# Row halves of the matrix array for the kv products, their turn and the turn of the feature sums; two closing adds on GpSimd; three gathers moved ahead of a scatter

## The chip, the cores and the metric

The kernel runs on one core of a Trainium2 chip. The metric is the device time of one execution in microseconds, less is better. The core has TensorE (PE for its products, PEld for its weight loads), VectorE (DVE), ScalarE (ACT), GpSimd (POOL) and SyncE (SP), each with its own instruction queue in order.

## The reference

Random feature attention over 8 batches, 8 heads, 576 positions and 64 columns a head, then a mixture of 8 experts that takes for each of the 4608 tokens the one with the largest cosine to the token.

```python
def phi(x):                                   # 128 features, cos and sin
    proj = np.einsum('bhsd,md->bhsm', x, omega)
    return np.concatenate([np.cos(proj), np.sin(proj)], axis=-1) / np.sqrt(m)
q_p, k_p = (phi(q), phi(k))
kv = np.einsum('bhsm,bhsd->bhmd', k_p, v)     # (features x 64) for each head
z = np.sum(k_p, axis=2)                       # sum of each feature over the positions
num = np.einsum('bhsm,bhmd->bhsd', q_p, kv)
den = np.einsum('bhsm,bhm->bhs', q_p, z)      # then clamped away from zero
x = num / den                                 # rows of 512, one for each token
...
logits = xn @ en.T / tau                      # cosine with 8 expert vectors
expert_idx = np.argmax(logits, axis=1)
out[mask] = gate_w[mask, None] * (np.maximum(x[mask] @ w1[e], 0.0) @ w2[e])
```

## The kernel before

**Attention.** It goes in 32 steps n = 0 to 31, each for one batch and two heads (hh = 0 in partitions 0 to 63, hh = 1 in 64 to 127). The 576 positions are 9 chunks of 64. Everything is float32 here. The order of the work in a step is written out by hand in the loop `for n in range(NS)`, and each engine follows it in order; a step's products for step n are mixed with the numerators of step n - 1 and the projections of step n + 1. TensorE's order in the loop is: `proj_q(n)` (L235, L244 and one block of L218), `z_turn(n-1)` (L340), `kv_turn(n-1)` (L326), `proj_k(n+1)` (L218), `num(n-1)` (L371), `turns(n)` (L181), `kv_products(n)` (L306).

`kv_products` multiplies v (64 positions x 64 columns, the loaded weights) with the sines and cosines of k (`sck`: 64 positions x features; sines in half 0, cosines in half 1). Head hh takes rows 64 hh to 64 hh + 63 of the array. Eight of the nine chunks take both halves in one product of 256 columns; even chunks go to output columns 0 to 63 of the array and odd ones to 64 to 127, so that the sum over all chunks is in two parts. The last chunk is split in products of 128 columns. VectorE copies the result from PSUM (`kv_copy`, L316, 128 x 512). `kv_turn` loads 128 x 128 of that copy as weights and multiplies by `rmat`, which adds the two parts and appends the products with the 8 expert vectors.

The feature sums z: GpSimd adds the chunks of each half in `zsum` (L293 on 128 x 512, L295 on 128 x 256), down to two blocks and the ninth chunk, and `z_turn` (L340) adds these three over the positions with products against a matrix of ones: three products of 128 rows for each half, accumulated, with one column of result for each head. `kv_out` (L350, L353) copies both results to SBUF for `num`.

ScalarE rounds, takes absolute values, sines and copies (L262, L273, L283, L204 or L209). VectorE takes the fractions (L266), the absolute value of q's (L277), the copies from PSUM and the division of `num` (`norm`), and pieces of the routing in the steps from 9 on (`pieces`). GpSimd takes `zsum`, the issue of one piece of the expert weights each step (`weights_in`, 32 pieces, L92 and L98), the cast of the result (`to_rows`, L403), sums and squares (`sums` L449, `squares` L408). SyncE issues the loads of q, k, v and the stores of the rows. Tiles with one buffer tie these together: the `zs` tile of `zsum` is free again when `z_turn` has read it, and `kv_products` writes to the PSUM region `kreg` that the projection of k for the next step was read from.

**Experts.** 43 blocks of 128 tokens, each of one expert. The first 11 blocks are made from the tokens of the first four batches while the attention still runs, the other 32 after all logits are known; the token numbers of these (`prm`, L737) are ready in block j = 7. In the loop over j, TensorE does `hidden(j+1)` (L882, 32 products), the turn of a gathered block (`turn_x`, L824) and `result(j)` (L903, 8 products). `result(j)` ends with the scatter of the block's rows to the output, an indirect DMA that GpSimd issues (L916) after ScalarE has scaled the rows (L915). `gather(t)` (L782) is an indirect DMA too, issued by GpSimd after that; in block 7 these are the gathers of blocks 11, 12 and 13.

Of the kernel before, what the change touches and what calls it, by code (L numbers as in the profile page):

```python
# [11 lines left out]
FP32 = mybir.dt.float32  # L12
# [5 lines left out]
ALU = mybir.AluOpType  # L18
# [10 lines left out]
def kernel(  # L29
# [12 lines left out]
    nc = tc.nc  # L42
# [6 lines left out]
    P = 128  # L49
# [5 lines left out]
    NCH = S // 64  # L55
# [8 lines left out]
    W = 64 + E + 1  # L64
# [56 lines left out]
    pref = persist.tile([P, E], BF16)  # L121
    tri = persist.tile([P, E, E], FP32)
    sm = persist.tile([P, 12, E], FP32)
    ones2 = persist.tile([P, 2], FP32)
    pio2 = persist.tile([P, 1], FP32)
    sel = persist.tile([P, SG, E], BF16)
    pm = persist.tile([P, SG], BF16)
# [4 lines left out]
    with tc.tile_pool(name="psA", bufs=1, space=PSUM) as psA, tc.tile_pool(  # L132
# [9 lines left out]
        st = {}  # L142
# [144 lines left out]
        def zsum(n, half):  # L287
            d = st[n]
            t = d["sck"][:, half]
            if half == 1:  # L290
                d["z"] = pa.tile([P, 6, P], FP32, tag="zs", name="zs", bufs=1)
            z = d["z"]
            nc.gpsimd.tensor_tensor(z[:, 0:4], t[:, 0:4], t[:, 4:8], ALU.add)  # L293
            r = z[:, 4 * half : 4 * half + 2]
            nc.gpsimd.tensor_tensor(r, z[:, 0:2], z[:, 2:4], ALU.add)  # L295
            d[f"z{half}"] = (r[:, 0], r[:, 1], t[:, 8])

        def kv_products(n):
            d = st[n]
            parts = [(c, c % 2, 0, 2) for c in range(NCH - 1)]  # L300
            parts += [(NCH - 1, half, half, half + 1) for half in range(2)]
            for c, grp, a0, a1 in parts:
                for hh in range(2):
                    r0 = 64 * hh
                    at = 512 * hh + P * a0
                    nc.tensor.matmul(  # L306
                        kreg[64 * grp : 64 * grp + 64, at : at + P * (a1 - a0)],
                        lhsT=d["v"][r0 : r0 + 64, c],
                        rhs=d["sck"][r0 : r0 + 64, a0:a1, KS[c]],
                        start=(c < 2),  # L310
                        stop=(c == NCH - 1),
                    )

        def kv_copy(n):
            t = pa.tile([P, 2, 2 * P], FP32, tag="kvT", name="kvT", bufs=1)
            nc.vector.tensor_copy(  # L316
                t, kreg[:, 0:1024].rearrange("p (h m) -> p h m", h=2)[:, :, 0 : 2 * P]
            )
            st[n]["kvT"] = t

        def kv_turn(n):
            b, i = steps[n]
            d = st[n]
            for hh in range(2):
                for half in range(2):
                    nc.tensor.matmul(  # L326
                        nm2[:, half, hh * W : hh * W + W - 1],
                        lhsT=d["kvT"][:, hh, half * P : half * P + P],
                        rhs=rmat[:, i, hh],
                        start=True,  # L330
                        stop=True,
                    )

        ZC = 486

        def z_turn(n):
            for half in range(2):
                parts = st[n][f"z{half}"]
                for j, z in enumerate(parts):
                    nc.tensor.matmul(  # L340
                        nm2[:, 0, ZC + 2 * half : ZC + 2 * half + 2],
                        lhsT=z,
                        rhs=ones2,
                        start=(j == 0),
                        stop=(j == len(parts) - 1),
                    )

        def kv_out(n):
            kv = pa.tile([P, 2, 2, W], FP32, tag="kv", name="kv", bufs=1)
            nc.vector.tensor_copy(  # L350
                kv[:, :, :, W - 1], nm2[:, 0, ZC : ZC + 4].rearrange("p (a h) -> p a h", a=2)
            )
            nc.vector.tensor_copy(  # L353
                kv[:, :, :, 0 : W - 1],
                nm2[:, :, 0 : 2 * W].rearrange("p a (h w) -> p a h w", h=2)[:, :, :, 0 : W - 1],
            )
            st[n]["kv"] = kv
# [118 lines left out]
        load_kq(-1)  # L476
        load_v(0)
        make_identity(nc, ident)
        nc.vector.memset(ones2, 0.0)
        for hh in range(2):  # L480
            nc.vector.memset(ones2[64 * hh : 64 * hh + 64, hh : hh + 1], 1.0)
        nc.vector.memset(half1, 0.5)
        nc.vector.memset(pio2, PI_2)
        for par in range(2):
# [524 lines left out]
        def weights_in(n):  # L1009
            if n < 4 * E:  # L1010
                emit_weight_piece(n)

        weights_in(0)
        for n in range(NS):
# [34 lines left out]
                whole_turns(n + 1, "k")  # L1049
            if n < NS:  # L1050
                zsum(n, 1)
                weights_in(n + 1)
                fold(n, "q")
                wave(n, "si", "k")
            if nx:
# [4 lines left out]
            if n < NS:  # L1060
                wave(n, "co", "q")
                zsum(n, 0)
            if nx:
                if pieces.get(n):
                    copy_kq(n)
                else:
                    copy_k(n)
                    copy_q(n)
                if n + 2 < NS:
                    load_kq(n + 1)  # L1070
# [52 lines left out]
        square_sums(NS - 1)  # L1123

        r2 = {}
        QUIET = 7

        def route_second_pe(j):
            if j == 1:
# [62 lines left out]
        for j in range(NBLK):  # L1192
# [8 lines left out]
                gate_end(t)  # L1201
            for t in gates_at.get(j, []):
                gate_shift(t)
            result(j)
            route_second_pe(j)
            for t in gathers_at.get(j, []):
                gather(t)


# [33 lines left out]
```

## Time and profile before

| what | value |
|---|---|
| time, median of 3 runs | 536.39 us (535.89 to 536.85) |
| time of the profiled execution | 535.86 us |
| its span, first to last instruction | 534.1 us |
| PE, PEld busy | 510.4, 409.6 us |
| DVE, ACT, POOL busy | 349.8, 356.3, 324.1 us |
| mean granted TensorE clock | 0.985 |

The profiled execution's time is 1.8 us more than its span. Busy time is the sum over all stages; the 32 steps of the attention, the 43 blocks of the experts and the change between them have different limits, so the rows below are cut by stage.

### The profile page before, as it was taken

To read this page: it belongs to the slowest core of one execution; us is meant where nothing else is said; L and a number is where in the kernel's file an instruction comes from. 1 tells how busy PE (TensorE), PEld (TensorE's weight loads), DVE (VectorE), ACT (ScalarE), POOL (GpSimd) and SP (SyncE) were. 2 spreads that over 40 slices of the span, in tenths; PEclk is the share of its full clock that TensorE was granted. 3 is DMA by queue.
4 is the path that set the end of the run, shared out by engine and by line. 5 is a ranking of instruction groups with operands and counts; after the bars stand their busy time and mean duration, and the time that the engine had idled before them with its cause. 6 is when DMAs were issued, how large, how long until landed. Compare 5 with 4: busy or idle time off the path is not lost.

```text
span 534.1 us, 17479 instructions
## 1 busy us (share of the span) xinstructions
PE 510.4 (96%) x7244; PEld 409.6 (77%) x7244; DVE 349.8 (66%) x756; ACT 356.3 (67%) x466; POOL 324.1 (61%) x374
## 2 busy tenths in 40 slices
PE   6799999999999999999999999989988999999993
PEld 4588888878888887888778878877766677777772
DVE  4468866786766688888878778858934444444440
ACT  5687877888788788878877888746633343333431
POOL 3357666665866566667677676876653655556422
PEclk9799999999999999999999999999998999999997
DMA  6655777677668858766866677524232323233110
GB/s 148 147 119 120 151 169 154 124 161 168 139 138 159 180 121 155 173 142 124 177 158 136 124 170 156 97 49 107 80 110 73 111 78 114 84 105 106 52 50 0
DMA packets 57885, 65.81 MB, mean 123 GB/s; under 512 B 29637, under 2 KB 37829, under 8 KB 57808
## 3 DMA queue, kind: packets, MB, share of 16 engines
q0 software_dynamic: 18304, 31.11, 29.0%
q1 hardware_dynamic: 39200, 33.51, 24.0%
q8 instruction: 58, 0.95, 0.7%
q14 instruction: 19, 0.16, 0.1%
q10 hardware_dynamic: 304, 0.08, 0.1%
HBM read 68.08 MB, written 16.16 MB: 158 GB/s over the span
## 4 chain that ended last, share of the span: by engine, by line
PE 87%; issue 4%; POOL 2%; ACT 2%; DVE 2%; another core or an unknown queue 1%; DMA 1%; POOLq 0%; ACTq 0%
PE ps L371 14%; PE ps L882 13%; PE ps L306 13%; PE ps L903 10%; PE ps L340 9%; PE ps L218 8%; PE ps L235 7%; PE ps L181 6%; PE ps L326 6%; PE ps L824 2%; POOL out_dram L916 1%; DMA w_sb<-in_omega_dram 1%; DVE sck L266 0%; ACT sck L283 0%
## 5 line engine op out<-in xcount | busy, mean ns | idle before, releaser
L293 POOL TENSOR_TENSOR zs<-sck 128x512 f32<-128x512 f32 x64 | 81.6, 1275 | 92.0 <-PE ps L326 58.7
L882 PEld LDWEIGHTS <-w_sb 128*128 x1376 | 81.7, 99 | 12.3 <-issue 3.2
L882 PE MATMUL ps<-kq,w_sb 128*128 128x128 f16 x1376 | 85.6, 221 | 1.8 <-DVE kq L818 1.0
L903 PE MATMUL ps<-w_sb,late 128*128 x344 | 81.9, 379 | 2.0 <-issue 2.0
L371 PE MATMUL ps<-kv,siq 128*64 128x73 f32 x1152 | 76.5, 229 | 0.8 <-DVE kv L353 0.6
L371 PE MATMUL ps<-kv,coq 128*64 128x73 f32 x1152 | 74.9, 226 | 0.0
L894 DVE TENSOR_SCALAR late<-ps 128x512 f16<-128x512 f32 x34 | 23.5, 692 | 69.2 <-PE ps L882 38.8
L371 PEld LDWEIGHTS ps<-kv,siq 128*64 128x64 f32 x1152 | 59.8, 135 | 4.8 <-ACT sck L283 0.8
L262 ACT ACTIVATE sck<-ps 128x1152 f32<-128x1152 f32 x32 | 36.2, 1132 | 37.8 <-issue 34.5
L371 PEld LDWEIGHTS ps<-kv,coq 128*64 128x64 f32 x1152 | 60.4, 137 | 0.0
L218 PEld LDWEIGHTS ps<-omT,kqT 64*128 64x128 f32 x576 | 45.1, 196 | 18.9 <-issue 15.6
L903 PEld LDWEIGHTS <-late 128*128 128x128 f16 x344 | 31.8, 98 | 33.1 <-issue 3.1
L782 POOL DMA_INDIRECT xin_all<-rf_x,prm x43 | 44.2, 1028 | 12.5 <-issue 9.8
L218 PE MATMUL ps<-omT,kqT 64*128 64x128 f32 x576 | 51.1, 292 | 0.6 <-DVE kqT L199 0.6
L295 POOL TENSOR_TENSOR zs<-zs 128x256 f32<-128x256 f32 x64 | 48.5, 758 | 5.0
L262 ACT ACTIVATE siq<-ps 128x1152 f32<-128x1152 f32 x32 | 36.2, 1130 | 17.8 <-PE ps L244 17.8
L266 DVE SCALAR_TENSOR_TENSOR siq<-siq,ps 128x1152 f32<-128x1152 f32 x32 | 43.0, 1345 | 2.9 <-ACT siq L262 2.9
L266 DVE SCALAR_TENSOR_TENSOR sck<-sck,ps 128x1152 f32<-128x1152 f32 x32 | 42.9, 1342 | 2.4 <-ACT sck L262 2.4
L916 POOL DMA_INDIRECT out_dram<-siq,prm x21 | 22.2, 1056 | 36.0 <-ACT siq L915 30.2
L916 POOL DMA_INDIRECT out_dram<-late,prm x22 | 23.8, 1081 | 32.7 <-ACT late L915 26.9
L306 PE MATMUL ps<-sck,v 64*64 64x256 f32 (+1 forms) x680 | 38.9, 373 | 2.9 <-ACT coq L283 1.8
L283 ACT ACTIVATE coq<-coq,pio 128x1152 f32<-128x1152 f32 x32 | 39.9, 1247 | 2.5 <-DVE coq L277 2.5
(191 smaller groups left out, 1093.4 us busy)
## 6 DMA issues: line engine op xcount, KB each, us to landing
w_sb<-in_moe_w_dram POOLq DMA_DIRECT2D x32, 512.0 KB
kq<-in_k_dram SPq DMA_DIRECT2D x64, 144.0 KB, 4.1
kq<-in_q_dram SPq DMA_DIRECT2D x64, 144.0 KB, 4.5
v<-in_v_dram SPq DMA_DIRECT2D x34, 144.0 KB, 4.6
rf_x<-xb SPq DMA_DIRECT2D x32, 144.0 KB, 4.2
xin_all<-in_v_dram SPq DMA_DIRECT2D x30, 144.0 KB, 3.7
xin_all<-rf_x,prm POOLq DMA_INDIRECT x43
out_dram<-late,prm POOLq DMA_INDIRECT x22
```

Of the source, the lines that this page charges most:

```text
L218: nc.tensor.matmul(kreg[:, s * P : s * P + P], lhsT=t[r0 : r0 + 64, j * P : j * P + P], rhs=omT[r0 : r0 + 64], start=True, stop=True,)
L262: nc.scalar.activation(si, REG[nm], AF.Copy, bias=CMAGIC, scale=1.0)
L266: nc.vector.scalar_tensor_tensor(out=si, in0=si, scalar=CMAGIC, in1=REG[nm], op0=ALU.subtract, op1=ALU.subtract)
L293: nc.gpsimd.tensor_tensor(z[:, 0:4], t[:, 0:4], t[:, 4:8], ALU.add)
L295: nc.gpsimd.tensor_tensor(r, z[:, 0:2], z[:, 2:4], ALU.add)
L306: nc.tensor.matmul(kreg[64 * grp : 64 * grp + 64, at : at + P * (a1 - a0)], lhsT=d["v"][r0 : r0 + 64, c], rhs=d["sck"][r0 : r0 + 64, a0:a1 ...
L340: nc.tensor.matmul(nm2[:, 0, ZC + 2 * half : ZC + 2 * half + 2], lhsT=z, rhs=ones2, start=(j == 0), stop=(j == len(parts) - 1),)
L371: nc.tensor.matmul(nm2[r0 : r0 + 64, a, (c - c0) * W : (c - c0) * W + W], lhsT=ph[:, s * P + r0 : s * P + r0 + 64], rhs=d["kv"][:, half, h ...
L782: ins = nc.gpsimd.indirect_dma_start(out=t, out_offset=None, in_=x_rows[:], in_offset=bass.IndirectOffsetOnAxis(ap=prm[:, j : j + 1], axis=0),
L882: nc.tensor.matmul(h_ps[:, f * P : f * P + P], lhsT=weights(k), rhs=d["xT"][:, c * P : c * P + P], start=(c == 0), stop=(c == 3),)
L903: nc.tensor.matmul(y_ps, lhsT=d["hT"][:, c * P : c * P + P], rhs=weights(NW1 + c), start=(c == 0), stop=(c == NW2 - 1),)
L916: ins = nc.gpsimd.indirect_dma_start(out=out[:], out_offset=bass.IndirectOffsetOnAxis(ap=prm[:, j : j + 1], axis=0), in_=y, in_offset=None ...
```

## The change

- `kv_products`: each half of the features is a product of its own, 128 columns wide, for all nine chunks; half 0 goes to output columns 0 to 63 and half 1 to 64 to 127. 36 products in place of 20, and the sum over the chunks is complete in PSUM.
- `kv_copy` copies 128 x 256 in place of 128 x 512. `kv_turn` takes 64 rows of it (one half) as weights, four products as before, each on one half of the array's rows.
- `zsum_tail`, new, on GpSimd: two adds on 128 x 256 that fold the two blocks and the ninth chunk of both halves into one block a half. `z_turn` then takes four products of 64 rows and one column in place of six of 128 rows and two columns, each for one head and one half. The ones are one column in place of two, set with one instruction in place of three.
- `weights_in(n+1)` is issued on GpSimd's queue behind the second `zsum` and the tail in place of behind the first `zsum`.
- In block j = 7 the gathers of blocks 11 to 13 are issued ahead of `result(7)`, and so of its scatter.

```diff
         def zsum(n, half):
             ...
             nc.gpsimd.tensor_tensor(r, z[:, 0:2], z[:, 2:4], ALU.add)
-            d[f"z{half}"] = (r[:, 0], r[:, 1], t[:, 8])
+
+        def zsum_tail(n):
+            z = st[n]["z"]
+            r = z[:, 0:5:4]
+            nc.gpsimd.tensor_tensor(r, r, z[:, 1:6:4], ALU.add)
+            nc.gpsimd.tensor_tensor(r, r, st[n]["sck"][:, :, 8], ALU.add)
 
         def kv_products(n):
             d = st[n]
-            parts = [(c, c % 2, 0, 2) for c in range(NCH - 1)]
-            parts += [(NCH - 1, half, half, half + 1) for half in range(2)]
-            for c, grp, a0, a1 in parts:
-                for hh in range(2):
-                    r0 = 64 * hh
-                    at = 512 * hh + P * a0
-                    nc.tensor.matmul(
-                        kreg[64 * grp : 64 * grp + 64, at : at + P * (a1 - a0)],
-                        lhsT=d["v"][r0 : r0 + 64, c],
-                        rhs=d["sck"][r0 : r0 + 64, a0:a1, KS[c]],
-                        start=(c < 2),
-                        stop=(c == NCH - 1),
-                    )
+            for c in range(NCH):
+                for half in range(2):
+                    for hh in range(2):
+                        r0 = 64 * hh
+                        nc.tensor.matmul(
+                            kreg[64 * half : 64 * half + 64, 512 * hh : 512 * hh + P],
+                            lhsT=d["v"][r0 : r0 + 64, c],
+                            rhs=d["sck"][r0 : r0 + 64, half, KS[c]],
+                            start=(c == 0),
+                            stop=(c == NCH - 1),
+                        )
 
         def kv_copy(n):
-            t = pa.tile([P, 2, 2 * P], FP32, tag="kvT", name="kvT", bufs=1)
+            t = pa.tile([P, 2, P], FP32, tag="kvT", name="kvT", bufs=1)
...
         def kv_turn(n):
             ...
+                    r0 = 64 * half
                     nc.tensor.matmul(
                         nm2[:, half, hh * W : hh * W + W - 1],
-                        lhsT=d["kvT"][:, hh, half * P : half * P + P],
-                        rhs=rmat[:, i, hh],
+                        lhsT=d["kvT"][r0 : r0 + 64, hh],
+                        rhs=rmat[r0 : r0 + 64, i, hh],
...
         def z_turn(n):
+            z = st[n]["z"]
             for half in range(2):
-                parts = st[n][f"z{half}"]
-                for j, z in enumerate(parts):
+                for hh in range(2):
+                    r0 = 64 * hh
                     nc.tensor.matmul(
-                        nm2[:, 0, ZC + 2 * half : ZC + 2 * half + 2],
-                        lhsT=z,
-                        rhs=ones2,
-                        start=(j == 0),
-                        stop=(j == len(parts) - 1),
+                        nm2[:, hh, ZC + half : ZC + half + 1],
+                        lhsT=z[r0 : r0 + 64, 4 * half],
+                        rhs=ones1[r0 : r0 + 64],
+                        start=True,
+                        stop=True,
                     )
...
                 zsum(n, 1)
-                weights_in(n + 1)
                 fold(n, "q")
...
                 zsum(n, 0)
+                zsum_tail(n)
+                weights_in(n + 1)
...
+            if j == FOUND:
+                for t in gathers_at[j]:
+                    gather(t)
             result(j)
             route_second_pe(j)
-            for t in gathers_at.get(j, []):
-                gather(t)
+            if j != FOUND:
+                for t in gathers_at.get(j, []):
+                    gather(t)
```

## Rows read from the trace of the kernel before

**Rows 1.** The page: span, and busy time of each engine.

```profile
span 534.1 us, 17479 instructions
...
PE 510.4 (96%) x7244; PEld 409.6 (77%) x7244; DVE 349.8 (66%) x756; ACT 356.3 (67%) x466; POOL 324.1 (61%) x374
```

**Rows 2.** Busy times in a window: steps 1 to 30, from `z_turn` to `z_turn`.

```profile
core 0: us, PE busy (x) PEld busy (x) DVE busy (x) ACT busy (x) POOL busy (x), PEclk, DMA share, GB/s
26.77:341.86 315.09, 313.96 (x4971) 262.44 (x4969) 241.54 (x390) 260.38 (x240) 213.41 (x245) 1.00 0.70 147
```

**Rows 3.** Timeline of one step: start us, us, engine, line, count [idle before].

```profile
253.23 2.17 PE L306 MATMUL ps<-sck,v 64*64 64x256 f32 x40
...
253.51 0.76 POOL L295 TENSOR_TENSOR zs<-zs 128x256 f32<-128x256 f32 x1
...
255.34 1.13 PE L235 MATMUL ps<-kqT,omT 64*128 64x512 f32 x4
...
255.77 0.68 DVE L316 COPY kvT<-ps 128x512 f32<-128x512 f32 x1
...
256.62 0.61 PE L340 MATMUL ps<-ones,zs 128*128 128x2 f32 x4
...
257.95 0.97 PEld L326 LDWEIGHTS ps<-rmat,kvT 128*128 128x128 f32 x8
...
259.00 1.16 PE L218 MATMUL ps<-omT,kqT 64*128 64x128 f32 x16
...
260.09 0.35 PE L371 MATMUL ps<-kv,siq 128*64 128x73 f32 x4
...
260.26 1.13 ACT L262 ACTIVATE sck<-ps 128x1152 f32<-128x1152 f32 x1 [1.19 <-issue]
...
263.67 0.66 PE L306 MATMUL ps<-sck,xin_all 64*64 64x256 f32 x8
```

**Rows 4.** Timeline of PE in two short windows inside one `proj_k`.

```profile
259.21 0.95 PE L218 MATMUL ps<-omT,kqT 64*128 64x128 f32 x14
...
259.55 0.61 PE L218 MATMUL ps<-omT,kqT 64*128 64x128 f32 x8
```

**Rows 5.** Timeline of PE in two short windows, end of one `kv_products`.

```profile
255.01 0.40 PE L306 MATMUL ps<-sck,v 64*64 64x128 f32 x8
...
255.12 0.29 PE L306 MATMUL ps<-sck,v 64*64 64x128 f32 x4
```

**Rows 6.** Groups by line on GpSimd: busy us, mean ns | idle before.

```profile
L293 POOL TENSOR_TENSOR zs<-sck 128x512 f32<-128x512 f32 x64 | 81.6, 1275 | 92.0 <-PE ps L326 58.7 <-ACT sck L283 33.0
L295 POOL TENSOR_TENSOR zs<-zs 128x256 f32<-128x256 f32 x64 | 48.5, 758 | 5.0
...
L449 POOL TENSOR_TENSOR la<-la,xa 128x72 f32<-128x72 f32 x24 | 8.4, 352 | 0.0
```

**Rows 7.** Busy times in windows of one step (columns as in rows 2).

```profile
152.00:162.44 10.44, 10.44 (x167) 8.73 (x165) 6.77 (x11) 8.84 (x8) 6.85 (x8) 1.00 0.68 146
...
278.69:289.13 10.44, 10.44 (x167) 8.73 (x166) 9.49 (x14) 8.83 (x8) 8.73 (x11) 1.00 0.68 133
```

**Rows 8.** Timeline of the last step, 31.

```profile
348.80 2.18 PE L306 MATMUL ps<-sck,v 64*64 64x256 f32 x40 [1.01 <-issue]
...
349.86 0.73 POOL L295 TENSOR_TENSOR zs<-zs 128x256 f32<-128x256 f32 x1
...
350.91 0.61 PE L340 MATMUL ps<-ones,zs 128*128 128x2 f32 x4
```

**Rows 9.** Timeline of expert blocks 7 to 10.

```profile
388.82 0.19 DVE L737 SCALAR_TENSOR_TENSOR prm<-xa 128x32 int32<-128x32 f32 x1
...
392.49 0.97 POOL L916 DMA_INDIRECT out_dram<-siq,prm  x1 [3.22 <-ACT siq L915]
...
393.11 1.89 PE L903 MATMUL ps<-w_sb,late 128*128 x8
...
394.84 1.95 PE L882 MATMUL ps<-kq,w_sb 128*128 128x128 f16 x32
...
401.29 0.60 ACT L890 ACTIVATE late<-ps 128x512 f16<-128x512 f32 x1 [4.50 <-remote]
...
402.54 3.24 PE L882 MATMUL ps<-kq,w_sb 128*128 128x128 f16 x32 [0.99 <-DVE kq L818]
```

More of the change, by code (lines that the diff above doesn't have):

```diff
@@ L123 @@
     sm = persist.tile([P, 12, E], FP32)
-    ones2 = persist.tile([P, 2], FP32)
+    ones1 = persist.tile([P, 1], FP32)
     pio2 = persist.tile([P, 1], FP32)
@@ L295, in zsum @@
             nc.gpsimd.tensor_tensor(r, z[:, 0:2], z[:, 2:4], ALU.add)
-            d[f"z{half}"] = (r[:, 0], r[:, 1], t[:, 8])
+        def zsum_tail(n):
[3 more added lines that the diff above has]
+            nc.gpsimd.tensor_tensor(r, r, st[n]["sck"][:, :, 8], ALU.add)
         def kv_products(n):
             d = st[n]
-            parts = [(c, c % 2, 0, 2) for c in range(NCH - 1)]
-            parts += [(NCH - 1, half, half, half + 1) for half in range(2)]
-            for c, grp, a0, a1 in parts:
-                for hh in range(2):
-                    r0 = 64 * hh
-                    at = 512 * hh + P * a0
-                    nc.tensor.matmul(
-                        kreg[64 * grp : 64 * grp + 64, at : at + P * (a1 - a0)],
-                        lhsT=d["v"][r0 : r0 + 64, c],
-                        rhs=d["sck"][r0 : r0 + 64, a0:a1, KS[c]],
-                        start=(c < 2),
-                        stop=(c == NCH - 1),
-                    )
+            for c in range(NCH):
[9 more added lines that the diff above has]
+                        )
         def kv_copy(n):
-            t = pa.tile([P, 2, 2 * P], FP32, tag="kvT", name="kvT", bufs=1)
+            t = pa.tile([P, 2, P], FP32, tag="kvT", name="kvT", bufs=1)
             nc.vector.tensor_copy(
-                t, kreg[:, 0:1024].rearrange("p (h m) -> p h m", h=2)[:, :, 0 : 2 * P]
+                t, kreg[:, 0:1024].rearrange("p (h m) -> p h m", h=2)[:, :, 0:P]
             )
@@ L350, in kv_out @@
             nc.vector.tensor_copy(
-                kv[:, :, :, W - 1], nm2[:, 0, ZC : ZC + 4].rearrange("p (a h) -> p a h", a=2)
+                kv[:, :, :, W - 1], nm2[:, :, ZC : ZC + 2].rearrange("p h a -> p a h")
             )
@@ L478 @@
         make_identity(nc, ident)
-        nc.vector.memset(ones2, 0.0)
-        for hh in range(2):
-            nc.vector.memset(ones2[64 * hh : 64 * hh + 64, hh : hh + 1], 1.0)
+        nc.vector.memset(ones1, 1.0)
         nc.vector.memset(half1, 0.5)
@@ L1125 @@
         r2 = {}
-        QUIET = 7
+        QUIET = FOUND = 7
         def route_second_pe(j):
```

## The prediction, made before the kernel ran

> **What bounds the kernel now.** I read the busy times first, by engine for the whole span and then for the window of the attention loop. TensorE is busy 510 of 534 us [rows 1], and 314.0 of the 315.1 us of the 30 steps between the first and the last `z_turn` of the loop [rows 2]; the next engine, ScalarE, has 260.4. A busy PE may still hide waits, so I then read the timeline of one step. From one `kv_products` to the next it is 263.67 - 253.23 = 10.44 us, and each group of products begins where the one before ends: `kv_products` 2.11, `proj_q` 1.28, `z_turn` 1.33, `kv_turn` 1.05, `proj_k` 1.09, the rest numerators and turns of q and k [rows 3]. The reader is to see that no group waits for data, while ScalarE does: it sits idle 1.19 us until `proj_k` has run. So a step is as long as TensorE's list, and what is taken off the list is a gain until the next engine is as long. The busy times of single steps tell where that is: in a light step VectorE has 6.77, ScalarE 8.84 and GpSimd 6.85 us, in the heaviest VectorE 9.49 and GpSimd 8.73 [rows 7].
>
> **The turns of the sums and of kv.** Now `z_turn` is 12 load-and-product pairs (a float32 product is two) in 1.33 us, 0.111 each, and `kv_turn` 8 in 1.05, 0.131 each with the change to the next group [rows 3]. A product of 2 columns and one of 72 cost nearly the same, so the load of 128 columns sets the pace. `proj_k` loads 128 columns too, but each product has one half of the rows and the halves alternate: six of its pairs start within 0.34 us, 0.057 each, even with 128 columns of data [rows 4]. Each of its two halves writes to a PSUM bank of its own; the changed turns alternate the halves in the same way, also with a bank for each half. So I price both by that row: 8 x 0.057 = 0.45 us each. `z_turn` falls by 0.88, `kv_turn` by 0.60, together 1.48 us a step. The low bound of the gain: if the halves did not run side by side, only the four pairs that are gone count, 4 x 0.111 = 0.44, and the change between groups 0.16, as both groups now have `proj_k`'s shape; 0.60 in all. I take 1.48, since `proj_k` is the same form.
>
> The Trainium skill (TensorE: Matmul & The Clock Gate, "LDWEIGHTS (loading the stationary operand)") says that a load's time goes with its columns and not with its rows. By that sentence alone halving the rows saves nothing and the sum would be that of the low bound; `proj_k`'s rows show what the halves give when they alternate.
>
> **kv products.** 20 products become 36, so 40 pairs become 72. The data columns stay: 16 x 256 + 4 x 128 = 4608 = 36 x 128. The row nearest to the new form is the old ninth chunk, four pairs of 128 columns on the four quarters of the array: the next four start 0.11 us after them [rows 5]. 18 such fours are 1.98 us, with the last one's run about 2.1, as now. From the other side, if the price went by the pair, 72 x 2.11 / 40 = 3.80, or +1.69 a step. I take 0; this is the edit whose upper bound eats all of the gain.
>
> **Copies and memsets.** VectorE's copy of 512 elements takes 0.68 us and would be done at 256.45, before `kv_turn` needs it at 257.95 [rows 3]. Half of it lies between 0.34 and 0.68; it is off the path, and in VectorE's heaviest step it is worth 0.2 to 0.3. Two memsets fewer at the start lie beside the first loads: 0.
>
> **GpSimd.** The tail adds two instructions on 128 x 256, as L295 at 0.758 us: 1.52 a step. The bounds are the 128 x 72 add (2 x 0.352 = 0.70) and the 128 x 512 add (2 x 1.275 = 2.55) [rows 6]; the shape is L295's, so I take that. What covers it: in the step shown the last `zsum` ends at 254.27 and `z_turn` reads it at 256.62, 2.35 us later [rows 3]; 0.8 is left. `weights_in` moves behind second `zsum` and tail, so one issue with its DMA leaves some 3 us later; nothing in the loop waits for expert weights. Queued behind it are the cast, the sums and the squares of the step before, whose readers are stores and VectorE's sums in later steps, and then the next `zsum`. So GpSimd's price is its total: 6.85 + 1.52 = 8.37 in a light step, below the 10.44 - 1.48 = 8.96 of TensorE; in a step with norms 8.73 + 1.52 = 10.25 [rows 7], and TensorE will wait for z there.
>
> The Trainium skill (SBUF — State Buffer, "SBUF: two separate sides") says that VectorE and GpSimd share a port pair that one instruction holds to its end. GpSimd's adds here come close together in duration, so the trace shows little of it now; with both engines fuller it would speak against this edit, as the rival below that GpSimd sets the step.
>
> **Sum over the loop.** 30 steps x 1.48 = 44.4 us. Some 18 steps carry routing pieces; there ScalarE (8.83) and VectorE (up to 9.49 - 0.25 = 9.24) are as long as the new list, and I estimate 0.3 us lost in each: 5.4. About three steps have GpSimd's norms: 10.25 against 8.96, of which a queue's slack takes a part, 1.0 each: 3. That leaves 36.0. In step 31 TensorE already waits 1.01 us for v, which is requested only when `kv_products(30)` frees its buffer; the shorter turns make that wait longer: 0. The last `z_turn` starts 0.32 us after GpSimd's last add (349.86 + 0.73 to 350.91) [rows 8]; the tail makes it wait 1.2 and the turns themselves give back 1.48: 0.
>
> **The gathers.** `prm` is ready at 389.01, but GpSimd is then waiting 3.22 us for block 7's result and issues that scatter at 392.49, with the three gathers behind it, and so five indirect DMAs and more stand one behind the other. Block 10's hidden products are through at 396.8 by their records, yet ScalarE gets to them only at 401.29, after 4.50 us for which the profile has no cause, and block 11's begin at 402.54 and take 3.24 in place of 1.95 [rows 9]. Without the pause they would have begun 1.7 us after 396.8, so it costs 4.0 and then 1.3. Ahead of the scatter the gathers go from 389 to 393 into GpSimd's idle time; scatter 7 follows about 0.8 us later than now, and only the store of its rows waits for it. That the crowd of DMAs makes the pause is a reading, no more: the gain lies between 0 and 5.3, and I take 4.
>
> **Total.** 36.0 + 4 = 40.0. Against the profiled execution's own 535.86 that gives 495.9; its time is 0.5 below the median of the runs, so 496.
>
> **The rivals.** (A) GpSimd sets the step. At the high bound of the tail it has 9.40 us in a light step, and it waits twice for ScalarE; with 0.4 for these the step is 9.8, the gain 30 x 0.64 = 19, with the gathers 23: 513. Against it: the shape is L295's. (B) The halves load one after the other: 0.60 a step, 18, with the gathers 22: 514. Against it: `proj_k`. (C) ScalarE and VectorE hand over more slowly than their busy time tells. ScalarE at 8.84 has nearly no slack and its waits for turns, `proj_q` and `proj_k` do not all vanish; at 9.6 a step the gain is 25, with the gathers 29: 507. (D) As forecast in the loop, but the pause stays or moves: 500. (E) Slower: `kv_products` go by the pair. At +1.69 against -1.48 a step, 30 x 0.21 = 6, less 4 for the gathers: 538. It turns at 1.48 + 4 / 30 = 1.61 a step more, so at 0.052 us a pair; the rows of the ninth chunk show 0.11 for four, 0.028 a pair. (F) Nothing comes of it, since some wait that the list hides takes its place: 536.
>
> **How the numbers follow.** The forecast has 0.50, D 0.15, C 0.12, A 0.10, B 0.08, E 0.03, F 0.02. The forecast's own range goes from 486 (no loss in heavy steps and all of the pause: 44.4 + 5.3 = 49.7) to 502 (the loss in heavy steps twice as large, half of the pause). For 8 in 10 it reaches to C and most of A and B: 485 to 513. A change of 0.2% (1 us) is about what a measurement of this kernel can tell from none. Faster has 0.95, same 0.02, slower 0.03.
>
> **What would show it.** In the profile of the changed kernel `z_turn` and `kv_turn` take about 0.45 us each from start to the next group's start; `kv_products` stay near 2.1 with 72 records; light steps are 8.9 to 9.1 us, heavy ones 9.2 to 9.5; ScalarE's wait for `proj_k` is gone. GpSimd's tail adds take 0.76, and its norms show up as a wait of `z_turn` for `zs`. The gathers of blocks 11 to 13 start as soon as `prm` is written, and the hole of 4.5 us on ScalarE is gone. Wrong would be a tail add over 1.2 us, turns at 0.11 a pair, `kv_products` over 2.5, or steps that stay near 10 with TensorE waiting.

## The result, and the profile after

The changed kernel takes 517.49 us (median of 4 runs, 516.16 to 523.92) where the kernel before takes 536.62 beside it: ratio 0.963, 95% interval 0.960 to 0.967. It is faster by 3.7%, less than half of the gain forecast, and the time lies above the range. The profiled execution took 517.76 us, of which the span is 515.9. The ratios, here and below, leave disturbed executions out, so one can differ from the ratio of the medians beside it.

The page: span and busy times.

```profile
span 515.9 us, 19333 instructions
...
PE 464.1 (90%) x8140; PEld 384.5 (75%) x8140; DVE 353.9 (69%) x754; ACT 353.0 (68%) x466; POOL 379.9 (74%) x438
```

TensorE lost 46 us of work and the span only 18: it waits now. Busy times in windows: the 30 steps that answer to [rows 2], then single steps (counted from 0 here, as in the expectations: step 7, then 8, 16 and 18 with routing pieces, then 22 and 23 with norms), and the last one, step 30, which the prediction calls 31.

```profile
core 0: us, PE busy (x) PEld busy (x) DVE busy (x) ACT busy (x) POOL busy (x), PEclk, DMA share, GB/s
22.62:322.72 300.10, 275.09 (x5811) 241.19 (x5808) 247.06 (x390) 256.78 (x240) 264.30 (x303) 0.98 0.73 155
...
88.67:97.87 9.20, 8.85 (x198) 7.79 (x196) 7.17 (x12) 8.24 (x8) 8.33 (x11) 1.00 0.75 159
...
97.87:110.53 12.66, 10.46 (x197) 9.40 (x195) 9.06 (x19) 8.80 (x8) 11.13 (x14) 0.87 0.59 112
176.79:189.33 12.54, 10.34 (x198) 9.28 (x195) 9.03 (x19) 8.81 (x8) 11.14 (x14) 0.86 0.60 120
198.78:212.41 13.63, 10.41 (x197) 9.29 (x195) 11.20 (x20) 8.80 (x8) 11.22 (x14) 0.87 0.65 118
...
241.46:254.00 12.54, 9.02 (x198) 7.77 (x194) 8.80 (x16) 10.94 (x10) 9.48 (x11) 1.00 0.69 162
254.00:264.44 10.44, 10.44 (x193) 9.33 (x195) 9.14 (x12) 6.64 (x6) 10.03 (x12) 0.84 0.45 93
...
322.72:335.49 12.77, 6.27 (x169) 5.69 (x166) 7.17 (x14) 6.92 (x6) 12.00 (x14) 0.95 0.46 88
```

The light step is 9.20, of which TensorE works 8.85 in the one shown and 8.84 in most; before, nearly all steps were 10.44 [rows 7], and the longest, which has norms, 11.64. But steps 8, 16 and 18, with routing pieces, are 12.5 to 13.6 us, longer than before. In these the granted clock also falls: in step 8 it is 0.53 from 102.02 to 105.50, that is the lower of the two levels (1.2 GHz) nearly throughout, after TensorE has stood for 2.20 us. The longest step before, and this stretch:

```profile
256.62:268.26 11.64, 10.51 (x168) 8.73 (x166) 8.59 (x17) 9.86 (x9) 8.47 (x10) 1.00 0.77 166
...
102.02:105.50 3.48, 3.48 (x60) 3.48 (x62) 3.45 (x3) 1.35 (x2) 3.25 (x4) 0.53 0.49 98
```

The waits of TensorE, longest sums first:

```profile
PE ps L309 <- ACT coq L283: 10.3, 22, 1.8
PE ps L345 <- POOL zs L301: 9.6, 3, 4.7
PE ps L376 <- DVE kv L358: 9.5, 6, 3.2
...
PE ps L309 <- issue: 3.4, 4, 1.1
```

Before, the same list has 1.8 us for coq, 1.1 for zs, 0.6 for kv and 1.0 for issue. What makes the waits is read from the timeline (start, duration, engine, line, [idle before]): a light step, a part of step 7, steps 8 and 18, a norm, the last `z_turn`, and the expert stage.

```profile
60.38 0.51 PE L345 MATMUL ps<-ones,zs 64*128 64x1 f32 x8
60.74 0.65 PE L330 MATMUL ps<-rmat,kvT 64*128 64x72 f32 x8
61.23 1.11 PE L218 MATMUL ps<-omT,kqT 64*128 64x128 f32 x16
...
91.55 1.64 DVE L277 TENSOR_SCALAR coq<-siq 128x1152 int32<-128x1152 int32 x1
...
92.66 1.13 POOL L295 TENSOR_TENSOR zs<-zs 128x256 f32<-128x256 f32 x1
...
93.12 1.34 DVE L266 SCALAR_TENSOR_TENSOR sck<-sck,ps 128x1152 f32<-128x1152 f32 x1
...
94.56 2.19 PE L309 MATMUL ps<-sck,v 64*64 64x128 f32 x72 [0.35 <-ACT coq L283]
...
98.90 0.34 POOL L454 TENSOR_TENSOR la<-la,xa 128x72 f32<-128x72 f32 x1
...
99.27 0.22 DVE L588 COPY lsq<-la 64x72 f32<-64x72 f32 x1 [1.78 <-POOL la L454]
...
102.02 0.37 PE L376 MATMUL ps<-kv,siq 128*64 128x73 f32 x4 [2.20 <-DVE kv L358]
...
200.07 1.35 DVE L634 TENSOR_SCALAR sm<-sm 128x8 f32<-128x8 f32 x1
...
200.25 1.14 POOL L413 TENSOR_TENSOR xa<-xa 128x576 f32<-128x576 f32 x1
...
201.43 1.26 POOL L293 TENSOR_TENSOR zs<-sck 128x512 f32<-128x512 f32 x1
201.46 1.26 DVE L635 TENSOR_SCALAR sm<-sm 128x8 f32<-128x8 f32 x1
...
203.95 0.35 PE L376 MATMUL ps<-kv,siq 128*64 128x73 f32 x4 [3.22 <-DVE kv L358]
...
247.80 2.03 POOL L440 TENSOR_TENSOR lsq<-lsq,half 128x9 f32<-128x9 f32 x1 [1.22 <-DVE lsq L434]
...
254.00 0.61 PE L345 MATMUL ps<-ones,zs 64*128 64x1 f32 x8 [3.17 <-POOL zs L301]
...
326.77 2.39 POOL L440 TENSOR_TENSOR lsq<-lsq,half 128x9 f32<-128x9 f32 x1
...
335.49 1.01 PE L345 MATMUL ps<-ones,zs 64*128 64x1 f32 x8 [4.72 <-POOL zs L301]
...
374.38 0.19 DVE L740 SCALAR_TENSOR_TENSOR prm<-xa 128x32 int32<-128x32 f32 x1
...
375.36 1.04 POOL L785 DMA_INDIRECT xin_all<-rf_x,prm  x1 [0.53 <-DVE xa L752]
...
379.74 0.69 ACT L918 ACTIVATE siq<-ps,gpos 128x512 f32<-128x512 f32 x1 [1.43 <-remote]
```

Light step: the turns are as forecast, `z_turn` 60.74 - 60.38 = 0.36 and `kv_turn` 0.49. Step 7: the fold of q (L277) takes 1.64 us beside GpSimd's adds; over the run its mean is 1565 ns where it was 1038 (lines below), and L295's is 928 where it was 758 [rows 6]. Step 8: VectorE's copy waits 1.78 us for GpSimd's logit sums, and `kv_out` stands behind it. Step 18: two VectorE instructions on 128 x 8 take 1.35 and 1.26 us; they end with the GpSimd instruction that runs beside them, 201.42 with 201.39 and 202.72 with 202.69. Before, when GpSimd was idle at that place, the same instructions took 0.17 each. The fold over the run, before and after, and the first of the two short instructions before:

```profile
L277 DVE TENSOR_SCALAR coq<-siq 128x1152 int32<-128x1152 int32 x32 | 33.2, 1038 | 1.1
...
L277 DVE TENSOR_SCALAR coq<-siq 128x1152 int32<-128x1152 int32 x32 | 50.1, 1565 | 1.1
...
215.54 0.17 DVE L631 TENSOR_SCALAR sm<-sm 128x8 f32<-128x8 f32 x1
```

Where the span's 18.2 us came from, by the same marks in both traces: up to the first `z_turn` 26.77 to 22.62, -4.15; the 30 steps 315.09 to 300.10, -15.0; the last step 9.05 to 12.77, +3.7; from there to the writing of `prm` 38.1 to 39.1, +1.0; from there to the end 145.1 to 141.3, -3.8.

### The profile page after: what moved, and what is told of

It reads as the page before. It is cut to its first block, busy times and chain, and to the rows that moved or that the text cites. A ratio compares the mean times of both kernels' runs of the same rounds, so it can differ in the third digit from the quotient of the medians.

```text
span 515.9 us, 19333 instructions
## 1 busy us (share of the span) xinstructions
PE 464.1 (90%) x8140; PEld 384.5 (75%) x8140; DVE 353.9 (69%) x754; ACT 353.0 (68%) x466; POOL 379.9 (74%) x438
## 4 chain that ended last, share of the span: by engine, by line
PE 49%; POOL 14%; DVE 14%; ACT 12%; issue 8%; DMA 1%; POOLq 0%; SPq 0%; ACTq 0%
PE ps L309 10%; PE ps L885 10%; PE ps L906 9%; ACT sck L283 5%; PE ps L218 5%; PE ps L376 5%; PE ps L235 5%; ACT coq L283 4%; POOL zs L293 3%; ACT sck L262 3%; POOL zs L295 2%; PE ps L330 2%; POOL xin_all L785 2%; PE ps L181 2%; DVE coq L277 2%
## 5 line engine op out<-in xcount | busy, mean ns | idle before, releaser
L376 PE MATMUL ps<-kv,siq 128*64 128x73 f32 x1152 | 82.4, 239 | 9.5 <-DVE kv L358 9.5
L376 PE MATMUL ps<-kv,coq 128*64 128x73 f32 x1152 | 81.0, 236 | 0.2 <-issue 0.2
L376 PEld LDWEIGHTS ps<-kv,siq 128*64 128x64 f32 x1152 | 65.6, 144 | 13.7 <-ACT sck L262 4.7
L376 PEld LDWEIGHTS ps<-kv,coq 128*64 128x64 f32 x1152 | 66.3, 145 | 0.3 <-issue 0.3
L295 POOL TENSOR_TENSOR zs<-zs 128x256 f32<-128x256 f32 x64 | 59.4, 928 | 5.0
L218 PEld LDWEIGHTS ps<-omT,kqT 64*128 64x128 f32 x576 | 44.0, 192 | 15.6 <-issue 14.5
L277 DVE TENSOR_SCALAR coq<-siq 128x1152 int32<-128x1152 int32 x32 | 50.1, 1565 | 1.1
L218 PE MATMUL ps<-omT,kqT 64*128 64x128 f32 x576 | 48.6, 282 | 0.6 <-DVE kqT L199 0.6
L309 PE MATMUL ps<-sck,v 64*64 64x128 f32 x1224 | 38.1, 272 | 9.9 <-ACT coq L283 6.8
L266 DVE SCALAR_TENSOR_TENSOR sck<-sck,ps 128x1152 f32<-128x1152 f32 x32 | 42.9, 1342 | 2.4 <-ACT sck L262 2.4
L266 DVE SCALAR_TENSOR_TENSOR siq<-siq,ps 128x1152 f32<-128x1152 f32 x32 | 43.0, 1343 | 1.8 <-ACT siq L262 1.8
```

The source lines that it names most:

```text
L218: nc.tensor.matmul(kreg[:, s * P : s * P + P], lhsT=t[r0 : r0 + 64, j * P : j * P + P], rhs=omT[r0 : r0 + 64], start=True, stop=True,)
L266: nc.vector.scalar_tensor_tensor(out=si, in0=si, scalar=CMAGIC, in1=REG[nm], op0=ALU.subtract, op1=ALU.subtract)
L277: nc.vector.tensor_scalar(co.bitcast(I32), si.bitcast(I32), 0x7FFFFFFF, None, ALU.bitwise_and)
L309: nc.tensor.matmul(kreg[64 * half : 64 * half + 64, 512 * hh : 512 * hh + P], lhsT=d["v"][r0 : r0 + 64, c], rhs=d["sck"][r0 : r0 + 64, hal ...
L376: nc.tensor.matmul(nm2[r0 : r0 + 64, a, (c - c0) * W : (c - c0) * W + W], lhsT=ph[:, s * P + r0 : s * P + r0 + 64], rhs=d["kv"][:, half, h ...
```

## The experiments

Theory Q is that GpSimd's longer list ate the gain. Rivals came from the prediction (H: the hand-overs of ScalarE and VectorE, or the new products) and from the trace (P, S, I and F, each told in the expectation where it first stands). Runs of one call share a chip. The kernel before took 528.9 to 530.3 us on the chips of most of them, so ratios and steps are compared; loop means the 30 steps.

**1. Each part alone, and the pieces moved.**

```diff
 e1: -  zsum_tail(n)                 # and z_turn, kv_out, ones as before
     +  weights_in(n + 1)            # behind the first zsum again
 e2: kernel before  +  zsum_tail, z_turn of four products, weights_in behind the tail
 e3: kernel before  +  gathers of block 7 ahead of result(7)
 e4: changed kernel
     -            piece_now(n)       # all pieces run in all_pieces(n), behind frac(k)
```

> The change without GpSimd's two tail adds: z_turn, its ones and the place of weights_in as before, the kv products, the kv turn and the order of the gathers as changed. Theory Q (GpSimd's longer list is what ate the gain: VectorE's routing pieces wait for its sums and behind its adds, kv comes late, TensorE pauses and its clock falls): the steps with routing pieces lose their waits of 2 to 3 us before the numerators, every step has the old z_turn again (1.33 in place of 0.36), so all steps stand near 8.84 + 0.97 = 9.8 us; the loop about 296 in place of 300, the last step 3 us shorter, the time about 510. Rival H (ScalarE's and VectorE's hand-overs set the loop, or the new kv products do, and the tail is covered): the waits stay and each step is 0.97 longer, the time about 545.

> The kernel before with the tail adds, the four-product z_turn and weights_in behind the tail, but the old kv products, kv turn and gathers. Theory Q: light steps 10.44 - 0.97 = 9.47, which gives 29 us over the loop, but the steps with routing pieces and norms lose some 18 of them, as in the changed kernel: about 525. Rival H (the tail is covered): nearly all of the 29 stays, about 508.

> The kernel before with nothing but the gathers of blocks 11 to 13 ahead of the scatter of block 7. If the crowd of indirect DMAs makes the pause of blocks 10 and 11, the time from the writing of prm to the end falls from 145 to about 141 us and the whole by 3 to 4, to about 533; if the pause has another cause, there is no change, 536.6.

> The changed kernel with one line taken out: VectorE runs no routing piece ahead of its square sums and kv_out, all of a step's pieces run behind the fraction of k. Theory Q: kv_out no longer stands behind instructions that wait for GpSimd; the waits before the numerators (2.2, 2.2, 3.2, 0.6, 0.6 us) go, and with them the low clock that follows them (some 5 us): about 505. If the slowed VectorE instructions cost as much in their new place (turns, norms of the numerators): about 512. Rival H: no change, 517.

Measured: e1 517.0 us, 0.975 (0.970 to 0.981); e2 515.9, 0.975 (0.969 to 0.981); e3 528.3, 0.997 (0.994 to 1.000); e4 516.7, 0.977 (0.971 to 0.983). A light step of e1 and of e2, by windows, and the steps 8, 16 and 18 of e4:

```profile
82.91:92.92 10.01, 10.01 (x200) 8.84 (x198) 7.25 (x11) 8.47 (x8) 6.85 (x9) 1.00 0.75 166
```

```profile
80.42:89.86 9.44, 9.44 (x166) 7.84 (x164) 7.33 (x12) 8.41 (x8) 8.70 (x11) 1.00 0.83 173
```

```profile
99.90:109.51 9.61, 9.21 (x197) 7.97 (x194) 8.28 (x16) 8.66 (x8) 9.05 (x11) 1.00 0.77 175
179.52:189.14 9.62, 9.01 (x198) 7.79 (x194) 8.29 (x16) 8.81 (x9) 9.06 (x11) 1.00 0.82 181
198.92:208.21 9.29, 8.98 (x198) 7.85 (x194) 8.71 (x17) 8.67 (x8) 8.21 (x10) 1.00 0.77 159
```

The kv part alone takes 0.43 off a step, where 0.60 was forecast for its turn, and its waits before the numerators are gone; the tail part alone takes 1.00 off, where 0.88 was forecast, with TensorE never idle in a light step. Both parts of Q hold: without the tail the piece steps are even (10.0), and with the pieces out of `kv_out`'s way the three long steps fall by 3 to 4 us each. H is out, since e1 without the tail has no such waits, and its 545 and 508 for e1 and e2 would be 1.016 and 0.947. Of the totals, e2's is the one that Q gives: 525 of 536.6 is 0.978, and 15.5 us of its loop (298.7 - 30 x 9.44) go to pieces and norms where Q had 18. e1 misses: its loop is 306.1 in place of 296, since a step is 10.0 where 9.8 was expected, and two with norms are 11.65 and 13.12. e4 misses too, 0.977 where Q's 505 to 512 are 0.941 to 0.954: its loop is 296.55 where the changed kernel has 300.10, but other waits came in, and steps 11 and 12 became 12.4 and 10.5.

The gathers give 0 to 0.6%. More telling, from `prm` to the end e2, with the old order of the gathers, takes 139.4 us, and e1, e3 and e4 take 139.3. The pause of [rows 9] was not there on that chip in either order, so the 3.8 us between the first two traces are not shown to be the reorder's.

**2. The order on each engine.**

```diff
 e5: changed kernel, unaltered
 e6: e4, and   -  norms(g)                      # GpSimd, inside the pieces
               +  norms(g) behind squares(n - 1); last inverse_norms behind kv_out(NS - 1)
 e7: e6, and   +  frac(n + 1, "k"); fold(n + 1, "k"); fold(n, "q")   # k first
               +  wave(n, "co", "q") behind the copies of the turns; z_turn behind kv_turn
 e8: changed kernel
               +  sums(n - 1); weights_in(n + 1); to_rows(n - 1)     # GpSimd: sums first
```

> The changed kernel, nothing altered, beside the variants on one chip. If the ratio to the kernel before is the 0.963 of its first timing, then it is 1.2% ahead of the variants with one part alone (both 0.975) and the two parts add up in some measure; if it is near 0.975 here, the two parts together give no more than either alone, as theory Q (GpSimd's list and VectorE's waits behind it eat what the second part frees) would have it. The light steps stand at 9.20 with 0.36 us of pause ahead of the kv products in either case.

> The kernel with the routing pieces behind the fraction of k, and besides GpSimd's norms (the power, 2.0 to 2.4 us, and the add) behind all its other work of the step in place of ahead of the second zsum; the inverse after the loop and its store move behind the last kv_out. Theory Q: the steps with norms (12.4 + 10.5 + 10.0 and 12.6 + 10.5 us in the kernel without this) lose about 3 us each time, as the power still costs its 2.3 us of GpSimd's time but no longer the wait for VectorE's square rows as well; the last z_turn comes 2.7 us earlier. Together 8 us: about 508 where the kernel without this has 516.7. Rival (these waits have nothing to do with the place of the norms): no change.

> As the kernel with the norms behind, and VectorE makes the fraction of k ahead of the fold of q, ScalarE the fold of k ahead of the waves of q, and z_turn goes behind kv_turn. Theory P (the fold of q takes 1.64 us in place of 0.98 since it shares something with GpSimd's adds, and what is late by it is the fraction of k, which frees the PSUM columns of the kv products: the pause of 0.36 us in each light step, which the profile puts down to ScalarE): the pause ahead of the kv products goes, light steps 8.85 to 8.95, 25 x 0.3 = 8 us less, about 501. Rival S (the pause is ScalarE's wave, as the profile says; the wave comes later still here): the pause stays or grows, light steps 9.2 to 9.8, 508 to 520.

> The changed kernel with one thing altered: GpSimd adds up the logit sums ahead of its weight issue and its cast, so 1.35 us earlier in its list. If only the order in GpSimd's list makes kv late (VectorE's copy of the sums waits 1.78 us for them in steps 8 and 16), these two steps fall from 12.6 to about 10.5 us and the clock hardly falls in them; step 18 (13.6 us), in which nothing waits for the sums, stays: 4 us in all, about 513. If VectorE's short instructions go on waiting behind whatever GpSimd runs at that time, steps 8 and 16 gain about 1 us each only, 2 us in all.

Measured: e5 520.7, 0.985 (0.979 to 0.990); e6 512.6, but from 502.6 to 518.3 in its four runs, so nothing is drawn from it; e7 514.0, 0.972 (0.965 to 0.978); e8 511.0, 0.964 (0.958 to 0.970). So on this chip the changed kernel is no faster than either part alone. Steps 8, 16 and 18 of e8, and a light step of e7:

```profile
100.41:110.21 9.80, 8.93 (x198) 7.88 (x195) 8.84 (x18) 8.84 (x8) 9.29 (x12) 1.00 0.71 152
176.49:186.19 9.70, 8.83 (x197) 7.78 (x195) 8.79 (x18) 8.80 (x8) 9.19 (x11) 1.00 0.76 159
195.64:205.76 10.12, 8.90 (x197) 7.81 (x195) 8.98 (x20) 8.77 (x8) 9.64 (x13) 1.00 0.73 141
```

```profile
167.30:176.07 8.77, 8.77 (x198) 7.76 (x197) 6.82 (x12) 8.07 (x9) 8.37 (x11) 1.00 0.75 156
```

One place in GpSimd's list is worth 9.2 us on these three steps against the first trace (38.83 - 29.62) and 6.4 against e5's on the same chip (35.99), more than was expected: also step 18, in which nothing waits for the sums, falls to 10.12, since the weight issue now comes before GpSimd's cast, so that VectorE's short instructions meet that cast and no longer the two long adds (there L634 takes 0.69, ending 0.03 after the cast, and L635 0.17). P holds against S: with the fraction of k ahead of the fold, the pause of 0.36 before the kv products is gone in light steps (8.8 to 9.1), though ScalarE's wave comes later: in the step shown the products start at 172.36 and the wave at 173.31. What the profile put down to ScalarE was VectorE's fraction, which frees the PSUM columns, late by the slowed fold. In e7 most steps from 8 on wait up to 1.5 us for VectorE's copy ahead of `kv_turn` instead, so its total gains little.

**3. Combined.**

```diff
 e9:  e8 + e7's order of fold, fraction and z_turn      e10: e9 + e6's norms
 e11: e8 + e6's norms
 e12: e10, and -  nc.gpsimd.tensor_tensor(r, r, st[n]["sck"][:, :, 8], ALU.add)
               +  for j, t in enumerate((z[:, 4 * half], ck[:, half, 8])):   # eight products
```

> The changed kernel with the logit sums ahead in GpSimd's list (511 alone) and the other order on VectorE and ScalarE (fraction of k ahead of the fold of q, fold of k ahead of the waves of q, z_turn behind kv_turn); the routing pieces are where they were. Theory Q + P: light steps 8.8 to 9.05 in place of 9.20, and without the late pieces the waits of kv_turn for VectorE's copy (0.7 to 1.5 us in some 12 steps of the run with pieces and fold moved) do not come: about 506. If those waits came from the new order and not from the late pieces: about 514.

> The same with GpSimd's norms behind its other work of the step and the last inverse behind kv_out. If the norms' 2.3 us of GpSimd's time is all that they cost, the two steps with norms lose 2 us each in place of 4.5, and the last z_turn comes 2.5 us earlier: 5 to 7 us less than with both orders alone, about 500. If only the last step gains: 2.5 us less.

> The changed kernel with the logit sums ahead and the norms behind, without the new order on VectorE and ScalarE. Theory Q: 5 to 7 us less than the 511 with the sums ahead alone, about 505; light steps still 9.20, as theory P holds their pause to come from the fold of q.

> As the kernel with both orders and the norms behind, but GpSimd leaves out the second tail add, and z_turn takes eight products (the last sums and the ninth slot, accumulated on the row parts). TensorE's list is 0.36 longer (8 pairs at 0.045), GpSimd's 0.81 shorter. If GpSimd's total still sets many steps (norms, weights, gathers), their waits for z go and it comes out even or up to 4 us faster; if not, it is 30 x 0.3 = 9 us slower.

Measured: e9 513.9, 0.968 (0.963 to 0.973); e10 515.2, 0.973 (0.969 to 0.977); e11 515.5, 0.977 (0.970 to 0.985); e12 514.0, 0.970 (0.967 to 0.974). None beats e8's 0.964. e9 comes out at its second number, but not by the waits named there: its light steps are down to 8.8 to 9.1, while TensorE waits 11.9 us for z in four steps and stands 11.0 inside the kv products (1.0 of it is the last step's wait for v). e10 and e11 miss: steps 12 and 23 are 15 to 16 us, because the inverse of the norms is one of the pieces ahead of `kv_out`, and with the power later VectorE waits for it. The timeline of e11, and its largest wait of TensorE:

```profile
143.71 0.22 DVE L445 RECIPROCAL lsq<-lsq 128x9 f32<-128x9 f32 x1 [5.42 <-POOL lsq L441]
```

```profile
PE ps L376 <- DVE kv L358: 12.5, 8, 4.4
```

It is the forecast's mistake again, in an experiment's expectation. e12 is even with e10, as its first branch has it: it has one add of 0.73 us less on GpSimd in each step, and light steps of 9.22 where e10's are 8.8 to 9.1. So neither list alone sets the time.

**4. What was open: the pauses in the kv products, the inverse, and whether the kv part pays.**

```diff
 f1: e11, and  -  lay(n + 4, [lambda: inverse_norms(0)], 1)    # and the same at n + 7
               +  lay(n + 4, [lambda: None, lambda: inverse_norms(0)], 2)
 f2: e2 + gathers + e8's order;  z_turn only where n == 1
 f3: e2 + gathers + all orders of f1         f4: e8 again
 g1: f3 again, g2: changed kernel, one chip, five rounds
```

> The changed kernel with the logit sums ahead, the norms behind GpSimd's other work, and the inverse of the norms moved behind the fraction of k in its step (it stood ahead of kv_out, where VectorE waited for the power and TensorE 4.2 and 4.4 us for kv). Theory Q: the two steps of 15.8 and 14.9 us fall to 9.2 to 10, with z late by 1 to 2 us in one step each; the loop about 288, the time about 4 us below the run with the sums ahead alone on this chip. If the power still holds TensorE up elsewhere, it is even with that run.

> The tail adds, the order of the gathers and the logit sums ahead, with the old 20 kv products and the old kv turn; z_turn is left out in all steps but the first, so that TensorE's list is 9.44 - 0.36 = 9.08 us. It leaves out the sums' turns, and their readers take old values. Theory I (the pauses inside the kv products come from the 16 more products a step, 32 loads and 32 products, since TensorE's instructions are fetched in pieces): no pause inside the kv products although the steps are as short as in the changed kernel. Rival F (fast steps crowd the transfers, and the fetch is late whatever the products): 2 to 5 us of such pauses, as in the changed kernel.

> The tail adds, the gathers and all three orders of the first kernel of this call, with the old kv products, copy and turn. If the kv part pays once GpSimd's and VectorE's orders are mended, this is 30 x 0.24 = 7 us slower than the first (9.44 against 9.20 a step); if the kv part costs in pauses and in a VectorE chain that is too tight what it saves, both are even.

> The changed kernel with the logit sums ahead alone, beside the others on one chip: 511 as before, 9 to 10 us below the changed kernel's 520.7.

> The kernel with the tail adds, the gathers and the three orders and with the old kv products, once more, beside the changed kernel on one chip: 507, ratio to the kernel before 0.955 to 0.965.

> The changed kernel on the same chip: between its two earlier ratios, 0.963 and 0.985; 8 to 12 us slower than the kernel with the old kv products and the three orders. Were the kv part worth its 13 us (30 steps of 0.43) here as well, it would be the other way round.

Measured: f1 511.0, 0.962 (0.956 to 0.968); f2 509.4 (one execution); f3 507.0, 0.959 (0.954 to 0.964); f4 513.4, 0.970 (0.964 to 0.976); g1 509.9, 0.950 (0.946 to 0.955); g2 522.2 (median of 7), 0.960 (0.954 to 0.966). The loops of f3 and f1 by windows, then f2's pauses inside the kv products (here L311):

```profile
23.96:313.34 289.38, 284.91 (x4850) 236.25 (x4847) 239.50 (x389) 260.58 (x240) 265.67 (x303) 1.00 0.78 161
```

```profile
24.89:321.73 296.84, 276.05 (x5810) 241.27 (x5808) 245.69 (x390) 256.83 (x240) 264.77 (x302) 0.98 0.76 157
```

```profile
PE ps L311 <- issue: 1.1, 1, 1.1
```

Theory I holds against F: most of f2's steps are 9.1 to 9.2 like the changed kernel's, and with the 20 old products it has no pause but the last step's wait of 1.1 for v; the changed kernel has 2.3 us beyond that one, e9 10.0. f1 is nearer to its second branch: its interval overlaps f4's and its loop is 296.84, not 288, since the two norms still cost; steps 12 and 13 are 10.77 and 10.45, because the power's 2 us make z late, and its last step is 10.34 in place of 12.74. f3's median is 4 us below f1's, but the intervals overlap, so the two are even by time, where steps 0.24 longer would have made f3 7 us slower. The traces, one execution each, show what makes up for it: in the loop of f3 TensorE is idle 289.38 - 284.91 = 4.5 us, in f1's 20.8. g1 and g2 stand 1.0% apart by the ratios, less than the 8 to 12 us expected and with intervals that just meet; with e5, e8 and f3 the direction is the same. So the tail part with the orders mended beats the kernel before by 4 to 5%, and the changed kernel by 1.0% on the one chip where both ran; the kv part, in this form, shows no gain beside it.

One of the pauses, in the run of the unaltered changed kernel: timeline of the kv products of step 6, and the transfers from 87.0 to 89.6.

```profile
86.94 0.82 PE L309 MATMUL ps<-sck,xin_all 64*64 64x128 f32 x21
89.59 0.86 PE L309 MATMUL ps<-sck,xin_all 64*64 64x128 f32 x18 [1.83 <-issue]
```

```profile
q1 hardware_dynamic: 275, 0.45, 65.0%
q8 instruction: 1, 0.02, 2.1%
```

TensorE has its data and stands between pair 54 and 55 of 72. The packet of instructions is moved from 87.30 to 88.18, amid the loads of q and k, and TensorE goes on 1.41 us after its end. The other traces bear this out: of 61 such pauses over 0.15 us in thirteen runs with the new products, the last step's left out, 60 end 1.26 to 1.57 us after the end of the last packet on this queue, which moves one every 6.7 us or so in the loop. Over a run it moved 58 packets before and 66 after, one for about 250 of TensorE's loads and products. That TensorE waits for its instructions is read from these times; no run changed the packets alone.

## Why the prediction failed, step by step

- **Turns of the sums and of kv: right.** 0.88 and 0.60 forecast; 1.33 - 0.36 = 0.97 and 1.05 - 0.49 = 0.56 measured [rows 3]. TensorE's list fell to 8.84, below the 8.96 of the sum. Rival B (halves one after the other) is out.
- **kv products: right in their time, not in their cost.** 2.12 for 72 pairs (94.56 to 96.68) against 2.11, so E is out; but the added instructions bring pauses of 2.3 us here and 10.0 in e9, which no step of the prediction had.
- **"So GpSimd's price is its total": this step failed.** The adds take 0.73 where 0.76 was forecast, and in a light step the total, 8.33, is below TensorE's list, yet GpSimd's idle stretches were the cover of other things. Four terms, against 30 x 8.84 = 265.2 of TensorE's list, make up the loop's 34.9 us of loss where 8.4 (5.4 for routing steps, 3 for norms) had been set aside, over a list of 8.96. (1) The fold of q runs beside GpSimd's adds, and the kv products start 0.36 late, counted in all steps: 30 x 0.36 = 10.8. (2) Steps 8, 16 and 18: 38.8 - 3 x 9.2 = 11.2, from late sums, slowed short instructions and the clock; 0.3 each had been forecast. (3) Norms: steps 11 and 12, 22 and 23, with 10.68 + 9.32 + 12.53 + 10.45 - 4 x 9.2 = 6.2; 3 had been forecast. (4) The rest, 6.7, in steps 2, 21, 25 and 29 mostly, where the kv products pause or wait. The first three have one root: the busy time of an engine was compared with the list of another, and nobody asked who is queued behind whom when the idle time goes. (The fourth is in part the pauses of the kv products.) The prediction had the reader of GpSimd's sums as "VectorE's sums in later steps"; that reader is a piece ahead of `kv_out`.
- **The row taken for the norms was another step's.** The 8.73 of GpSimd in [rows 7] has no norms in it. A step with norms is the one of 11.64 shown above, with 8.47 on GpSimd, and there TensorE already waited 1.13 us for z before the change: so the tail's 1.5 us could only lengthen it (3.17 after).
- **Shared port.** What rows show here: 128 x 8 instructions end 0.03 us after the GpSimd instruction beside them, and the fold rises from 1.04 to 1.57 us. The Trainium skill (SBUF — State Buffer, "SBUF: two separate sides") says that VectorE and GpSimd share a port pair which one instruction holds to its end while the other waits; the trace agrees, 1.35 in place of 0.17. The prediction weighed this rule only as a rival in which GpSimd's total sets the step (A); the total did not, the waits of single instructions did. The trace before had signs of it: in the very step of that 8.73, one of GpSimd's adds (L295, at 286.03) took 1.20 us beside VectorE's L708, where most took 0.73.
- **Last step: forecast 0, measured +3.7.** The norms' power (2.39) stands ahead of `zsum` there, and z comes 4.72 us late. With the norms behind, the last step is 10.3 (e10, e11, f1).
- **Gathers: forecast -4, not shown.** They start 0.8 us after `prm` is written, nearly as forecast, and the hole of 4.5 us on ScalarE shrank to 1.43; scatter 7 leaves 2.65 us later after `prm` than before, where 0.8 was forecast. But e2 has no such hole with the old order, and the gathers alone (e3) give 0 to 0.6%. What made it on the first chip stays open, and that -3.8 is so near to -4 is luck as far as the runs show.
- **Ahead of the loop: -4.15, not forecast.** `kv_products` and `proj_q` there ran at a granted clock of 0.53 before and 1.00 after. The same program (e8 and f4) has its first `z_turn` at 25.09 and 22.58, so some 2.5 us of this is chance.
- The four together: -15.0 in the loop for -36 (to which step 31 and the stretch from there to `prm` add +3.7 + 1.0 for 0), -3.8 for -4, -4.15 for 0: -18.2 for -40.0.

## What to carry to other kernels

Before work is put on an engine that looks idle, list what is queued behind it in each kind of step and who waits for that, and what the idle stretch shelters on the engine that shares its port; the total of busy times says neither. Price a step by its worst kind, not by the light one: three steps of thirty took back 11 of the 44 us that the shorter list was to bring. And when two changes each pay alone, time them together against one alone on one chip before both are kept.

## What the runs showed of the hardware

- VectorE instructions of 0.17 us took up to 1.35 us, ending with the GpSimd instruction beside them, while the fraction, which reads PSUM (L266), kept its 1.34 us beside the same adds.
- TensorE seems to run out of instructions in this unrolled code: pauses of 0.2 to 2.4 us inside 72 pairs of products whose data are there, 60 of 61 of them ending 1.26 to 1.57 us after an instruction packet, in steps of 8.8 to 9.2 us with 36 kv products; none with 20 products in steps as short (f2), none with 36 in steps of 10.0 (e1). The Trainium skill (Runtime: NRT & Kernel Launch, "Instruction fetch mechanics") calls the cost of such a refill mostly hidden; if these pauses are refills, here it is not, 1.83 us in the one shown.
- In steps 8, 16 and 18 the granted clock fell to the lower level after pauses of TensorE of 2.2 to 3.2 us, in step 8 for some 3.5 us, which added 1.5 to 1.6 us of busy time to each; pauses of up to 1.0 in e8's same steps left it at 1.00. The length of the pause does not settle it: after one of 2.29 us inside the kv products of e4's step 25 it stayed at 1.00.
